# Gated attention and Mish MLP on one core: dense products as four tiles of 32 weight columns instead of one of 128

## The chip, the cores and the metric

The kernel runs on one core of a Trainium2 chip. The metric is device time in microseconds (us) of one execution, as the median over several runs. A core has TensorE (PE in the profile), VectorE (DVE), ScalarE (ACT), GpSimd (POOL) and SyncE (SP, which here issues DMAs). TensorE multiplies a stationary operand, which a weight load brings in, with a moving operand, and writes to eight banks of PSUM; VectorE and ScalarE read PSUM.

## What is computed

One token sequence of S = 2048 with D = 640 goes through 32-head attention (20 numbers a head, no mask) and through a two-layer MLP with Mish (F = 1536). A gate from a dot product mixes the two.

```python
g = _sigmoid((x * gate_w).sum(-1, keepdims=True))
qkv = x @ wqkv                      # split into q, k, v of 32 heads of 20
p = softmax(q @ k.T * 20 ** -0.5)   # per head, 2048 x 2048
a = (p @ v, heads side by side) @ wo
h = x @ w1 + b1
b = (h * tanh(softplus(h))) @ w2    # Mish
return g * a + (1 - g) * b
```

(The lines are condensed; shapes are x 2048x640, wqkv 640x1920, wo 640x640, w1 640x1536, w2 1536x640, all bf16.)

## The kernel before

**Groups and scores.** The attention is cut into 32 groups: a group is one set of four heads (eight of these) by one block of 512 queries (four of these). A group has 16 key tiles of 128 keys. The scores of one head, one key tile and one query block are one matmul of 32 rows (20 used) by 128 keys by 512 queries, one PSUM bank large (`score`, line 1081). The four heads stand at four row positions of the array, so up to four such matmuls run beside each other: the array is used as four tiles of 32 rows. There are 2048 of them.

**Exponentials.** Most score tiles go to ScalarE, two or three banks in one instruction, which writes bf16 into the ring `E` (line 1131). For some key tiles VectorE makes the exponential instead: from a score it computes an integer that is read as bf16 (`power`, line 444, one per head), and two shifted copies of that (`shift`, line 468, one instruction for four heads). The three are averaged by the product with V: the shifted copies meet V times a constant (`VD`, made on line 385 for the last `ND` key tiles). Such a key tile, a "D set", costs VectorE four powers and two shifts, and takes two ScalarE instructions' worth of work away.

**Product with V.** The probabilities of one key tile times V are four matmuls (`emit_pv`, line 1174), one per head: 128 keys by 21 columns of V (20 and a one for the row sum) by 512 queries. They stand at four column positions, so the array is used as four tiles of 32 columns. All accumulate in bank 7. A plain key tile has one such set of four, a D set three. The same tiling is used by filler matmuls with zero weights (`heat`, line 1410), which the planner puts where it finds TensorE idle and its recent activity low.

**Dense products.** The Q and K projections (`dense_chain`, line 577; `first_k_mm`, line 552), V with the gate (`v_chain`, line 662), the MLP's first layer (`h_chain`, line 724) and second layer (`b_chain`, line 789) and the output projection (`wo_chain`, line 870) use the whole 128x128 array: one weight load of 128 columns and one matmul of 81, 240, 320 or 512 moving columns for each 128 of contraction. Each is cut into a chain of such pieces into one free PSUM bank, followed by an evacuation on VectorE. A `Chain` has a start and a due time in units of groups. Mish runs on ScalarE in two large instructions (line 776).

**Order.** All instructions are issued in an order that a planner in the kernel writes out while it is built. It keeps a clock for each of PE, ACT and DVE with costs for each operation (`MM` = 216 ns for a matmul of 512 columns, `SWITCH` = 100 ns for a change of kind on TensorE). At each step `step_pe` chooses between scores (S, from `emit_s` and `d_unit`), a V set (`go_v`), a piece of a dense chain (`go_f`), filler (`heat`) and nothing. `mode` holds the kind that TensorE did last, and `switch` charges `SWITCH` for any other kind. Limits such as how many D sets may be ahead (`LEAD`), how many V sets must be ready (`VMIN`, `PVMAX`), how far behind its due work the dense part may fall (`BEHIND`), or the activity under which filler is put in (`HEAT`) come from `rule`, and `PLAN` sets them anew for each of the 32 groups. `NTS` counts the buffers for D sets and their shifts. The order is fixed in the program: on the chip each engine goes through its list and waits on semaphores.

```python
if mode[0] == kind or mode[0] is None:
    return 0.0
return SWITCH
```

**Tail.** After the last V set, bank 7 is transposed on VectorE and normalised (lines 1195 to 1222), 24 matmuls finish the last four output tiles (line 1573), and four stores end the kernel.

Of the kernel before, what the change touches and what calls it, by code (L numbers as in the profile page):

```python
# [20 lines left out]
class Chain:  # L21


    def __init__(self, start, due, pieces, evac, ready=None, before=None):
        self.start, self.due = start, due
        self.pieces = deque(pieces)
        self.evac = evac
        self.ready = ready or (lambda t: True)
        self.before = before
        self.cost = sum(c for c, _ in pieces)  # L30
# [32 lines left out]
def kernel(  # L63
# [36 lines left out]
    ND = 6  # L100
# [4 lines left out]
    VDUE = 0.13  # L105
    VA0 = 0.8
    VA1 = 0.8
    VB0 = 0.0
# [5 lines left out]
    OC = 1.6  # L114
    OD = 2.6
    OA = 1.4
# [4 lines left out]
    NTS = 9  # L121
# [36 lines left out]
    rule.HROOM = 0.0  # L158
    rule.WAIT1 = 0.0
# [3 lines left out]
        0.0: {'AHEAD': 5000.0, 'D2': 0.5, 'DQ': 1, 'DQ3': 2, 'DQ4': 2, 'ETIGHT': 0, 'HEAT': 0.9, 'LEAD': 6, 'LOW': 0.5, 'MARGIN': 30.0, 'NOPEN': 3, 'PVMAX': 4, 'Q3': 2, 'ROOM': 200.0, 'SWTH': 380.0, 'VMIN': 3, 'WAIT1': 2000.0, 'WAIT2': 6000.0, 'WAITU': 0.0},  # L163
        1.0: {'DQ': 1, 'DQ3': 2, 'HROOM': 0.0, 'LEAD': 5, 'WAIT1': -2000.0},
        2.0: {'DQ': 2, 'DQ3': 2, 'DQ4': 0, 'ETIGHT': 1, 'HEAT': 0.7, 'HROOM': 0.0, 'LOW': 0.38, 'MARGIN': 0.0, 'NOPEN': 3, 'Q3': 3, 'VMIN': 3, 'WAIT1': 2000.0, 'WAIT2': 100000.0},
        3.0: {'AHEAD': 1000.0, 'D2': 0, 'DQ3': 3, 'DQ4': 2, 'ETIGHT': 1, 'HROOM': -100.0, 'LEAD': 6, 'NOPEN': 3, 'WAIT1': 2000.0},
        4.0: {'AHEAD': 1000.0, 'ETIGHT': 1, 'HEAT': 0.8, 'HROOM': 100.0, 'KEEP3': 2, 'LOW': 0.56},
        5.0: {'AHEAD': 5000.0, 'D2': 0.5, 'DQ': 1, 'DQ3': 1, 'DQ4': 3, 'HEAT': 0.8, 'HROOM': 100.0, 'LEAD': 6, 'LOW': 0.56, 'MARGIN': 30.0, 'NOPEN': 4, 'PVMAX': 4, 'Q3': 3, 'SWTH': 380.0, 'WAIT1': 0.0, 'WAIT2': 6000.0},
        6.0: {'AHEAD': 5000.0, 'DQ3': 3, 'DQ4': 3, 'ETIGHT': 0, 'MARGIN': 100.0, 'NOPEN': 3, 'WAIT1': 0.0, 'WAIT2': 30000.0},
        7.0: {'DQ': 1, 'DQ3': 2, 'DQ4': 2, 'ETIGHT': 0, 'HEAT': 0.8, 'LOW': 0.6, 'MARGIN': 0.0, 'NOPEN': 3, 'ROOM': 300.0, 'SWTH': 300.0, 'WAIT1': 0.0, 'WAIT2': 100000.0},  # L170
        8.0: {'AHEAD': 2000.0, 'BEHIND': 6000.0, 'D2': 0.5, 'HEAT': 0.9, 'LOW': 0.44, 'NOPEN': 4, 'SWTH': 380.0, 'WAIT1': 2000.0, 'WAIT2': 30000.0},
        9.0: {'AHEAD': 2000.0, 'BEHIND': 6000.0, 'D2': 1.0, 'DQ3': 0, 'DQ4': 0, 'ETIGHT': 0, 'LOW': 0.56, 'MARGIN': 0.0, 'ROOM': 200.0, 'WAIT2': 100000.0},
        10.0: {'AHEAD': 5000.0, 'D2': 0.5, 'DQ3': 1, 'DQ4': 1, 'ETIGHT': 0, 'KEEP3': 3, 'LOW': 0.41, 'PVMAX': 3, 'SWTH': 520.0, 'WAIT1': -2000.0, 'WAIT2': 6000.0, 'WAITU': 0.0},
        11.0: {'D2': 0.5, 'DQ': 1, 'DQ3': 2, 'HEAT': 0.8, 'NOPEN': 4, 'PVMAX': 2, 'Q3': 2, 'VMIN': 3, 'WAIT1': 0.0, 'WAITU': 0.0},
        12.0: {'AHEAD': 1000.0, 'DQ': 1, 'DQ3': 3, 'DQ4': 0, 'HEAT': 0.9, 'MARGIN': 0.0, 'Q3': 2, 'ROOM': 200.0, 'SWTH': 520.0, 'WAIT2': 100000.0},
        13.0: {'AHEAD': 2000.0, 'BEHIND': 3000.0, 'DQ3': 2, 'ETIGHT': 0, 'HEAT': 0.8, 'KEEP3': 2, 'LOW': 0.47, 'PVMAX': 3, 'SWTH': 380.0, 'WAIT2': 6000.0, 'WAITU': 0.0},
        14.0: {'AHEAD': 2000.0, 'BEHIND': 2000.0, 'D2': 0, 'DQ4': 3, 'ETIGHT': 0, 'HEAT': 0.7, 'MARGIN': 60.0, 'WAIT1': -2000.0, 'WAIT2': 3000.0},
        15.0: {'AHEAD': 5000.0, 'D2': 0.5, 'DQ': 1, 'DQ3': 2, 'DQ4': 1, 'ETIGHT': 0, 'HEAT': 0.9, 'HROOM': 0.0, 'KEEP3': 1, 'LOW': 0.53, 'MARGIN': 60.0, 'NOPEN': 4, 'PVMAX': 2, 'SWTH': 380.0, 'WAIT2': 6000.0},
        16.0: {'AHEAD': 1000.0, 'D2': 1.0, 'DQ': 1, 'DQ3': 3, 'HEAT': 0.9, 'LEAD': 6, 'MARGIN': 30.0, 'PVMAX': 3, 'Q3': 2, 'SWTH': 380.0, 'WAITU': 0.0},
        17.0: {'AHEAD': 1000.0, 'D2': 0.5, 'DQ': 2, 'DQ4': 0, 'HEAT': 0.8, 'KEEP3': 3, 'LEAD': 6, 'NOPEN': 4, 'ROOM': 100.0},  # L180
        18.0: {'AHEAD': 2000.0, 'D2': 0.5, 'DQ': 1, 'DQ3': 0, 'DQ4': 3, 'HROOM': 0.0, 'LEAD': 6, 'LOW': 0.38, 'MARGIN': 0.0, 'PVMAX': 2, 'Q3': 3, 'ROOM': 200.0, 'SWTH': 380.0, 'VMIN': 3, 'WAIT2': 6000.0},
        19.0: {'BEHIND': 6000.0, 'DQ': 1, 'DQ3': 0, 'ETIGHT': 0, 'HROOM': 100.0, 'LEAD': 4, 'LOW': 0.38, 'MARGIN': 0.0, 'NOPEN': 4, 'ROOM': 300.0, 'WAIT1': -2000.0, 'WAIT2': 6000.0, 'WAITU': 0.0},
        20.0: {'AHEAD': 1000.0, 'BEHIND': 4000.0, 'DQ': 1, 'DQ3': 0, 'DQ4': 3, 'HROOM': 0.0, 'KEEP3': 2, 'LEAD': 5, 'LOW': 0.41, 'MARGIN': 30.0, 'NOPEN': 4, 'PVMAX': 3, 'ROOM': 200.0, 'SWTH': 380.0, 'VMIN': 3, 'WAIT1': -2000.0},
        21.0: {'AHEAD': 5000.0, 'D2': 1.0, 'DQ': 1, 'DQ4': 0, 'ETIGHT': 1, 'LOW': 0.5, 'ROOM': 100.0, 'WAIT1': -2000.0, 'WAIT2': 100000.0, 'WAITU': -200000.0},
        22.0: {'AHEAD': 5000.0, 'D2': 1.0, 'HEAT': 0.8, 'KEEP3': 3, 'LOW': 0.41, 'PVMAX': 2, 'Q3': 3, 'WAIT1': 0.0, 'WAIT2': 3000.0},
        23.0: {'AHEAD': 1000.0, 'BEHIND': 4000.0, 'D2': 0.5, 'DQ': 1, 'DQ3': 0, 'DQ4': 3, 'LOW': 0.53, 'NOPEN': 4, 'PVMAX': 3, 'SWTH': 380.0, 'VMIN': 3, 'WAIT1': -2000.0, 'WAIT2': 30000.0},
        24.0: {'AHEAD': 3000.0, 'DQ': 2, 'DQ3': 1, 'ETIGHT': 1, 'KEEP3': 3, 'LOW': 0.6, 'NOPEN': 4, 'PVMAX': 2, 'Q3': 2, 'SWTH': 380.0, 'WAIT1': 0.0, 'WAIT2': 30000.0, 'WAITU': -200000.0},
        25.0: {'DQ': 2, 'DQ3': 2, 'DQ4': 2, 'ETIGHT': 0, 'KEEP3': 3, 'LEAD': 6, 'LOW': 0.56, 'MARGIN': 100.0, 'NOPEN': 3, 'PVMAX': 3, 'WAIT1': -2000.0, 'WAIT2': 30000.0, 'WAITU': 0.0},
        26.0: {'AHEAD': 3000.0, 'BEHIND': 4000.0, 'D2': 0, 'DQ': 2, 'ETIGHT': 1, 'MARGIN': 0.0, 'NOPEN': 4, 'WAITU': 0.0},
        27.0: {'D2': 1.0, 'DQ': 2, 'DQ4': 1, 'HEAT': 0.8, 'HROOM': -200.0, 'KEEP3': 1, 'LOW': 0.6, 'MARGIN': 100.0, 'ROOM': 100.0, 'WAIT2': 30000.0, 'WAITU': 0.0},  # L190
        28.0: {'AHEAD': 1000.0, 'D2': 0.5, 'DQ': 1, 'HEAT': 0.8, 'HROOM': 0.0, 'LEAD': 5, 'LOW': 0.6, 'MARGIN': 30.0, 'ROOM': 300.0, 'VMIN': 3, 'WAIT1': 0.0, 'WAIT2': 30000.0, 'WAITU': -200000.0},
        29.0: {'AHEAD': 1000.0, 'HEAT': 0.9, 'HROOM': 100.0, 'LOW': 0.6, 'ROOM': 300.0, 'VMIN': 3, 'WAITU': -200000.0},
        30.0: {'AHEAD': 5000.0, 'BEHIND': 4000.0, 'D2': 1.0, 'DQ': 1, 'DQ3': 0, 'HEAT': 0.9, 'KEEP3': 3, 'LOW': 0.6, 'NOPEN': 4, 'PVMAX': 3, 'ROOM': 100.0, 'SWTH': 300.0, 'VMIN': 3, 'WAIT2': 100000.0, 'WAITU': -200000.0},
        31.0: {'AHEAD': 3000.0, 'HEAT': 0.9, 'KEEP3': 2, 'LOW': 0.6, 'PVMAX': 3, 'ROOM': 100.0},
# [305 lines left out]

    def transpose_chain(s, start, due):
# [20 lines left out]
        return Chain(start, due, [(420.0, piece)], evac, lambda t: t >= ARRIVE[c])  # L522
# [28 lines left out]
    def first_k_mm(ps, kt, c):  # L551
        nc.tensor.matmul(
            ps[:, :],
            lhsT=wkp[:, kt, :, :].rearrange("p h d -> p (h d)"),
            rhs=xT[:, kt, c * QC : (c + 1) * QC],
            start=(kt == 0),
            stop=(kt == KT - 1),
        )
# [10 lines left out]
    def dense_chain(kind, i, c, start, due):  # L569
# [4 lines left out]
        def piece(kt, t):  # L574
            if kt == 0:
                box["ps"] = bank_tile([P, QC])
            nc.tensor.matmul(  # L577
                box["ps"][:, :],
                lhsT=strips[(kind, i)][:, kt, :],
                rhs=xT[:, kt, c * QC : (c + 1) * QC],  # L580
                start=(kt == 0),
                stop=(kt == KT - 1),
            )
            if kt == KT - 1:
                strip_left[(kind, i)] -= 1
                if strip_left[(kind, i)] == 0 and i + 2 < 4 + (kind == 0):
                    load_strip(kind, i + 2, nc.sync)
# [67 lines left out]
    def v_chain(sts, w, c0, n, start, due, gate=False):  # L655
        width = n + (1 if gate else 0)

        def piece(k, t):
            i, kt = divmod(k, KT)
            if k == 0:  # L660
                box["ps"] = bank_tile([P, len(sts), width])
            nc.tensor.matmul(  # L662
                box["ps"][:, i, :],
                lhsT=xT[:, kt, sts[i] * P : (sts[i] + 1) * P],
                rhs=w[:, kt, c0 : c0 + width],
# [51 lines left out]
    def h_chain(ft, c, start, due):  # L717
        def piece(kt, t):
            if kt == 0:
# [4 lines left out]
            nc.tensor.matmul(  # L724
                box["ps"][:, :],
                lhsT=w1t[NW1 * c + ft // W1N][:, kt, (ft % W1N) * P : (ft % W1N + 1) * P],
                rhs=xT[:, kt, c * QC : (c + 1) * QC],
# [267 lines left out]
    def pick(t, any_start=False):  # L995
# [3 lines left out]
        for k, ch in enumerate(chains):  # L999
            if (any_start or ch.start <= prog[0]) and ch.ready(t):  # L1000
# [3 lines left out]
                if ch.before:  # L1004
                    ch.before()
# [624 lines left out]
```

## Time and profile before

| | us |
|---|---|
| median of 3 runs (lowest, highest) | 740.72 (740.61, 746.36) |
| the profiled execution | 739.59 |
| its span, first to last instruction | 737.8 |
| dense products, busy TensorE (by line: 789, 724, 577, 662, 870, 552) | 74.5, 65.0, 48.9, 34.0, 31.7, 4.0 |
| VectorE powers (line 444), 552 instructions | 363.7 |
| VectorE shifts (line 468), 276 instructions | 183.0 |
| Mish (line 776), 2 instructions, ScalarE | 20.9 |

The profile is of one execution. Busy time counts a stretch once in which instructions of one engine overlap; an instruction's mean duration is longer than the distance to the next one where they are pipelined, as matmuls (382 ns long, 216 ns apart) and exponentials are. A few per cent of the matmul records are missing: 204 of the 240 matmuls of line 724 are there, for instance. So counts are taken from the program and distances from pieces of the timeline that are whole.

### The profile page before, as it was taken

How to read it: one execution, taken by the hardware profiler on the slowest of the kernel's cores; microseconds unless marked ns; L12 is line 12 of the kernel's file. 1: busy time of each engine (PE TensorE's matmuls, PEld its weight loads, DVE VectorE, ACT ScalarE, POOL GpSimd, SP SyncE). 2: the span in 40 equal slices, each digit the busy share in tenths (PEclk: the TensorE clock that was granted, in tenths of full speed). 3: DMA queues.
4: the chain of work that ended last, by engine and by line, in shares of the span. 5: the costliest groups of instructions: out<-in, count | busy, mean ns of one | idle time of the engine just before them, and what ended most of it. 6: DMA issues, size and time to landing. Idle time of an engine off the chain costs nothing.

```text
span 737.8 us, 17000 instructions
## 1 busy us (share of the span) xinstructions
PE 714.6 (97%) x6669; PEld 231.8 (31%) x6725; DVE 664.8 (90%) x1180; ACT 718.0 (97%) x753; POOL 5.2 (1%) x12
## 2 busy tenths in 40 slices
PE   8999999999999999999999999999999999999996
PEld 4433222222222333333323222222233333333332
DVE  4488999998998899999888999999998999989986
ACT  5899999999999999999999999999999999999995
POOL 2000000000000000000000000000000000000000
PEclk9999999999999999999999999999999999999999
DMA  9511221224111210101221223311111212213231
GB/s 250 168 23 31 49 43 36 48 42 110 30 41 31 65 35 15 16 14 35 54 82 33 40 48 84 76 41 24 34 34 55 56 28 63 48 32 79 43 89 46
DMA packets 125584, 39.99 MB, mean 54 GB/s; under 512 B 91136, under 2 KB 124944, under 8 KB 125504
## 3 DMA queue, kind: packets, MB, share of 16 engines
q1 hardware_dynamic: 123616, 38.05, 22.7%
q8 instruction: 52, 0.85, 0.5%
q10 hardware_dynamic: 1888, 0.86, 0.4%
q14 instruction: 28, 0.23, 0.1%
HBM read 23.61 MB, written 12.79 MB: 49 GB/s over the span
## 4 chain that ended last, share of the span: by engine, by line
PE 46%; ACT 38%; issue 8%; DVE 5%; DMA 2%; SPq 1%; ACTq 0%; DVEq 0%
ACT E L1131 36%; PE Sp L1081 17%; PE Sp L1174 14%; PE Sp L789 6%; PE Sp L577 2%; DVE T L444 2%; PE Sp L724 2%; PE Sp L870 2%; ACT big L776 1%; DVE T L468 1%; PE Sp L662 1%; SPq L839 1%; DMA q_dram<-st 1%; DMA od<-o_dram 1%; DMA bl<-b_dram 0%
## 5 line engine op out<-in xcount | busy, mean ns | idle before, releaser
L1131 ACT ACTIVATE E<-Sp 128x1024 bf16<-128x1024 f32 (+1 forms) x737 | 686.9, 1123 | 4.6 <-PE Sp L1081 4.4
L444 DVE TENSOR_SCALAR T<-Sp 128x512 int16<-128x512 f32 x552 | 363.7, 681 | 37.3 <-PE Sp L1081 33.6
L1081 PE MATMUL Sp<-qT,kT 32*128 32x512 bf16 x2048 | 298.1, 383 | 8.5 <-ACT E L1131 2.8
L468 DVE TENSOR_SCALAR T<-T 128x2048 int16<-128x2048 int16 x276 | 183.0, 677 | 0.8 <-PE Sp L1174 0.4
L1081 PEld LDWEIGHTS <-kT 32*128 32x128 bf16 x2048 | 82.2, 91 | 276.6 <-issue 272.1
L1174 PE MATMUL Sp<-E,VA 128*21 128x512 bf16 x1496 | 137.7, 382 | 0.0
L1174 PE MATMUL Sp<-T,VD 128*21 128x512 bf16 x1104 | 102.4, 382 | 0.4 <-DVE T L468 0.3
L789 PE MATMUL Sp<-w_sb,big 128*128 128x320 bf16 x384 | 74.5, 302 | 0.0
L724 PE MATMUL Sp<-xT,w1t 128*128 128x512 bf16 x204 | 65.0, 383 | 4.0 <-issue 3.7
L1174 PEld LDWEIGHTS <-VA 128*21 128x21 bf16 x2048 | 41.2, 90 | 60.2 <-issue 48.9
L1174 PE MATMUL Sp<-T,VA 128*21 128x512 bf16 x552 | 51.7, 383 | 0.0
L577 PE MATMUL Sp<-xT,ws 128*128 128x512 bf16 x162 | 48.9, 383 | 1.6 <-issue 1.4
L789 PEld LDWEIGHTS <-big 128*128 128x128 bf16 x384 | 28.4, 97 | 33.4 <-issue 27.4
L743 DVE TENSOR_SCALAR big<-Sp,b1f 128x512 bf16<-128x512 f32 x48 | 35.4, 738 | 1.0 <-PE Sp L724 0.9
L1174 PEld LDWEIGHTS <-VD 128*21 128x21 bf16 x1104 | 26.2, 90 | 30.1 <-issue 22.9
L662 PE MATMUL Sp<-wv,xT 128*128 128x81 bf16 (+2 forms) x240 | 34.0, 258 | 0.7 <-DVE T L444 0.5
L870 PE MATMUL Sp<-wo_sb,od 128*128 128x320 bf16 (+1 forms) x152 | 30.5, 302 | 0.8 <-DVE big L890 0.4
L597 DVE CAST st<-Sp 128x512 bf16<-128x512 f32 x36 | 24.5, 682 | 4.4 <-DMA q_dram<-st 2.8
L1195 DVE STREAM_TRANSPOSE T<-Sp 128x512 f32<-128x512 f32 x32 | 22.7, 708 | 2.3 <-PE Sp L1174 2.3
L724 PEld LDWEIGHTS <-w1t 128*128 128x128 bf16 x240 | 15.5, 97 | 29.0 <-issue 26.5
L678 DVE CAST VA<-Sp 128x80 bf16<-128x80 f32 (+2 forms) x48 | 16.1, 372 | 8.6 <-PE Sp L662 8.6
L662 PEld LDWEIGHTS <-xT 128*128 128x128 bf16 x240 | 16.5, 98 | 16.7 <-issue 14.5
(69 smaller groups left out, 194.4 us busy)
## 6 DMA issues: line engine op xcount, KB each, us to landing
w1t<-in_B_w_dram SPq DMA_DIRECT2D x24, 320.0 KB
q_dram<-st SPq DMA_DIRECT2D x20, 128.0 KB
b_dram<-bt SPq DMA_DIRECT2D x16, 160.0 KB
bl<-b_dram SPq DMA_DIRECT2D x16, 160.0 KB
qT<-q_dram SPq DMA_DIRECT2D x124, 20.0 KB
o_dram<-T SPq DMA_DIRECT2D x120, 20.0 KB
kT<-k_dram SPq DMA_DIRECT2D x28, 80.0 KB
out_dram<-ot SPq DMA_DIRECT2D x14, 160.0 KB
```

The costliest lines, as they stand in the source:

```text
L444: nc.vector.tensor_scalar(out=d["T"][:, r * QC : (r + 1) * QC].bitcast(I16), in0=ps[:, :], scalar1=inv_sqrt_dh * LOG2E * 128.0, scalar2=12 ...
L468: nc.vector.tensor_scalar(out=tile_[:, :].bitcast(I16), in0=d["T"][:, :].bitcast(I16), scalar1=float(SHIFT[i]), scalar2=None, op0=ALU.add,)
L577: nc.tensor.matmul(box["ps"][:, :], lhsT=strips[(kind, i)][:, kt, :], rhs=xT[:, kt, c * QC : (c + 1) * QC], start=(kt == 0), stop=(kt == K ...
L597: nc.vector.tensor_copy(out=res["st"][:, :], in_=ps[:, :])
L662: nc.tensor.matmul(box["ps"][:, i, :], lhsT=xT[:, kt, sts[i] * P : (sts[i] + 1) * P], rhs=w[:, kt, c0 : c0 + width], start=(kt == 0), stop ...
L724: nc.tensor.matmul(box["ps"][:, :], lhsT=w1t[NW1 * c + ft // W1N][:, kt, (ft % W1N) * P : (ft % W1N + 1) * P], rhs=xT[:, kt, c * QC : (c + ...
L743: nc.vector.tensor_scalar(out=big[:, slot.tag, (ft % 2) * QC : (ft % 2 + 1) * QC], in0=ps[:, :], scalar1=b1f[:, ft : ft + 1], scalar2=None ...
L789: nc.tensor.matmul(box["ps"][:, :], lhsT=big[:, pair[(c, ft // 2)].tag, (ft % 2) * QC + u * P : (ft % 2) * QC + (u + 1) * P], rhs=w2_sb[:, ...
L870: nc.tensor.matmul(box["ps"][:, :], lhsT=od[c][0:r, k, u * P : (u + 1) * P], rhs=wo_sb[0][0:r, k, cols], start=(k == 0), stop=(k == n - 1),)
L1081: nc.tensor.matmul(ps_cols, lhsT=kT[p][32 * t_ : 32 * t_ + 32, j * P : (j + 1) * P], rhs=qT[G][32 * t_ : 32 * t_ + 32, :], tile_position=( ...
L1131: nc.scalar.activation(E[:, x : x + n, :], ps, ACT.Exp, scale=inv_sqrt_dh,)
L1174: nc.tensor.matmul(acc[32 * t_ : 32 * t_ + DH + 1, :], lhsT=lhsT, rhs=rhs, start=(pv_done[G] == 0), stop=(pv_done[G] == pv_total[G] - 1), ...
```

## The change

Each dense product is made of four matmuls at column positions 0, 32, 64 and 96, each with 32 columns of the weights and the same moving operand, as the V sets are. The six places that issued one matmul call the new `product`. The initial projections (line 1275), the transposes and the 24 matmuls of the tail keep the whole array; so the transposes' chain gets `col=False`.

The planner now keeps two things: the kind it did last, and the tiling that the array has (`tiles`). A dense piece and a V set have the same tiling and cost no switch between them; where both could go on, it prefers the kind it is in. The costs of the pieces in the planner are what they were. Some constants and the table `PLAN` are new: one fewer key tile per group has a `VD`, there is one more buffer for D sets, and starts and due times of a few chains move. `rule.VF` is 0 throughout. `before` of `Chain` was not used and goes.

```diff
-    ND = 6
+    ND = 5
...
-    VDUE = 0.13
+    VDUE = 0.16
...
-    VB0 = 0.0
+    VB0 = 0.5
...
-    OC = 1.6
-    OD = 2.6
-    OA = 1.4
+    OC = 0.8
+    OD = 1.8
+    OA = 1.2
...
-    NTS = 9
+    NTS = 10
...
+    rule.VF = 0
...
+    def product(out_, lhsT, rhs, **kw):
+
+        for k in range(0, P, 32):
+            nc.tensor.matmul(
+                out_[k : k + 32], lhsT=lhsT[:, k : k + 32], rhs=rhs, tile_position=(0, k), **kw
+            )
+
...
-            nc.tensor.matmul(
+            product(
                 box["ps"][:, :],
-                lhsT=big[:, pair[(c, ft // 2)].tag, (ft % 2) * QC + u * P : (ft % 2) * QC + (u + 1) * P],
-                rhs=w2_sb[:, ft, half * HALF : (half + 1) * HALF],
+                big[:, pair[(c, ft // 2)].tag, (ft % 2) * QC + u * P : (ft % 2) * QC + (u + 1) * P],
+                w2_sb[:, ft, half * HALF : (half + 1) * HALF],
                 start=(ft == 0),
                 stop=(ft == FT - 1),
             )
...
-    M1 = 30.0
+    M1 = 31.0
...
+    tiles = [None]
+
+    def tiling(kind):
+        if kind == "F":
+            return "V" if chain[0] is None or chain[0].col else "F"
+        return kind
+
     def switch(kind):
-        if mode[0] == kind or mode[0] is None:
-            return 0.0
-        return SWITCH
+        return 0.0 if tiles[0] in (None, tiling(kind)) else SWITCH
+
+    def enter(kind):
+        sw = switch(kind)
+        mode[0], tiles[0] = kind, tiling(kind)
+        return sw
...
         if units:
-            if mode[0] == "V" and n_pv and slack > MM:
-                return go_v()
-            if mode[0] == "F" and slack > MM and can_f(slack):
-                return go_f()
+            if slack > MM and mode[0] in ("V", "F"):
+                if n_pv and tiles[0] == "V" and (mode[0] == "V" or rule.VF):
+                    return go_v()
+                if can_f(slack) and switch("F") == 0.0:
+                    return go_f()
+                if n_pv and tiles[0] == "V":
+                    return go_v()
...
-        if mode[0] == "V" and n_pv:
+        if n_pv and tiles[0] == "V" and (mode[0] == "V" or rule.VF):
             return go_v()
         if end and n_pv and cur["G"] >= NG - 1:
             return go_v()
-        if mode[0] == "F" and can_f(slack):
+        if mode[0] in ("V", "F") and can_f(slack) and switch("F") == 0.0:
             return go_f()
+        if n_pv and tiles[0] == "V":
+            return go_v()
```

## The prediction

> **What bounds the kernel now.** I read the page first: how full each engine is, and the chain of waits.
>
> ```profile
> span 737.8 us, 17000 instructions
> PE 714.6 (97%) x6669; PEld 231.8 (31%) x6725; DVE 664.8 (90%) x1180; ACT 718.0 (97%) x753; POOL 5.2 (1%) x12
> PEclk9999999999999999999999999999999999999999
> PE 46%; ACT 38%; issue 8%; DVE 5%; DMA 2%; SPq 1%; ACTq 0%; DVEq 0%
> ```
>
> ScalarE and TensorE are both at 97%, and the chain goes to and fro between them. DVE has 73 us free, and the clock stands at full. A busy PE is not a PE at its peak, so I take distances from the timeline, in a stretch in mid-kernel where no record is missing (start, length, engine):
>
> ```profile
> 299.74 6.59 ACT L1131 ACTIVATE E<-Sp 128x1024 bf16<-128x1024 f32 x7
> ...
> 299.97 0.39 PE L1081 MATMUL Sp<-qT,kT 32*128 32x512 bf16 x2
> ...
> 300.29 0.40 PE L1174 MATMUL Sp<-E,VA 128*21 128x512 bf16 x4
> 300.30 0.10 PEld L1174 LDWEIGHTS <-VD 128*21 128x21 bf16 x4
> 300.51 0.39 PE L1174 MATMUL Sp<-T,VD 128*21 128x512 bf16 x4
> ...
> 300.73 0.39 PE L1174 MATMUL Sp<-E,VA 128*21 128x512 bf16 x4
> ...
> 301.05 0.39 PE L1081 MATMUL Sp<-qT,kT 32*128 32x512 bf16 x3
> ...
> 301.38 0.58 PE L789 MATMUL Sp<-w_sb,big 128*128 128x320 bf16 x3
> ...
> 303.08 0.72 PE L789 MATMUL Sp<-w_sb,big 128*128 128x320 bf16 x4
> ...
> 303.73 0.39 PE L1081 MATMUL Sp<-qT,kT 32*128 32x512 bf16 x3
> ```
>
> Seven exponentials span 6.59 us and the last takes 1.11, so their distance is (6.59 - 1.11)/6 = 0.913. Four matmuls of a V set run together, and set follows set at 0.22 (0.216 between the second and third of a stretch). From scores to V is 0.32, from V to scores 0.32 as well: 0.216 of work and 0.105 lost at a change of tiling. From a product back to scores, 303.08 to 303.73, is 0.65 for four pieces; pieces of 320 follow each other at (0.72 - 0.30)/3 = 0.14 (0.136 in the records), so 0.10 is lost there. A last view, the groups by shape, has the sizes of the exponentials:
>
> ```profile
> L1131 ACT ACTIVATE E<-Sp 128x1024 bf16<-128x1024 f32 x715 | 661.6, 1110 | 4.1 <-PE Sp L1081 3.9
> L1131 ACT ACTIVATE E<-Sp 128x1536 bf16<-128x1536 f32 x22 | 33.8, 1534 | 0.5 <-PE Sp L1081 0.5
> ```
>
> **The reserve of each engine before.** ScalarE runs exponentials from 10.6 to 727.7, 717.1 us. At 0.913, and 0.42 more for each wide one, 737 take 682; Mish with its table loads 26. So ScalarE loses only 9 us to waits.
> For PE I count the program's order: 748 stretches of scores x 0.321 = 240.1; 788 V and 48 filler sets x 0.216 = 180.6; 339 ways out of V x 0.105 = 35.6; products 435 x 0.216 + 616 x 0.136 + 80 x 0.102 + 80 x 0.040 = 189.2 (512, 320, 240, 81 columns); 409 ways out of products x 0.096 = 39.3; 6.5 for first sets, which are 7 to 10 ns longer; 3.4 of transposes. Together 694.7 of the 718.1 us from the first scores (10.2) to the end of the last V set: a reserve of 23 us, 3%, some 5 of it in the first 20 us. PE is nearly as tight as ScalarE.
>
> **The change, part by part.** Instructions are counted from the two built programs.
>
> *Exponentials.* 715 narrow and 22 wide become 700 and 28: nine fewer x 0.913, less six x 0.42 = **-5.7 us** of ScalarE. D sets go from 138 to 141 (powers 552 to 564, shifts 276 to 282).
>
> *VectorE.* 12 x 0.66 + 6 x 0.67 = +12 us on 664.8: 677 of some 733. Its 56 us of free time cover it; uncovered it would cost those 12. The smaller `VD` tiles (16 of 0.28) give back under 1. Nothing.
>
> *Tiling changes.* Products and V sets now stand next to each other 98 times instead of 18. But scores still come between most stretches, and all changes of tiling fall only from 1519 to 1476: 13 fewer stretches of scores, -4.2 us. The ways out of products now cost what they cost from V: 728 x 0.105 and 0.7 for transposes, against 35.6 + 39.3 before, +2.2. First sets -1.4.
>
> *V and filler.* 794 V sets, +1.3 us; 75 fillers, +5.8.
>
> *Products as four tiles.* 1211 pieces become 4844 matmuls, each with its own weight load. For 512 columns the V set is the row: 0.216, what the whole-array piece takes too. So nothing for 435 pieces. For 320, 240 and 81 no row has four tiles. From below: the moving columns alone, as today, +0 (a gain is excluded, as a piece can't stream in less than its columns). From above: eight instructions in a row, one load and one matmul at the closest distance that the trace shows kept up, 0.040 (pieces of 81 columns: eight in 0.48, the last 0.20). Four pairs are 0.156 to 0.160: +20 ns x 616, +54 x 80, +116 x 80 = 12.3 + 4.3 + 9.3 = +26 us. I take +0 to +3: in a V set the four matmuls start 3 ns apart, so pairs can be issued far closer than 40 ns, and the row of four loads at 300.30 ends within 0.10, under the 0.136 of a piece of 320. Only the 80 pieces of 81 columns, before 50 us, should get longer.
>
> [...]
>
> *PE in all.* -4.2 + 2.2 - 1.4 + 1.3 + 5.8 = +3.7: 698.4 us with products as long as before.
>
> *Tail.* Before, the last exponential (726.6 to 727.7) ends just ahead of the last V set (728.12), and the end comes 10 us later. In the new order a power (0.66), two shifts (1.3) and a V set (0.4) stand behind the last exponential's start: some 2.9 us to the transpose of bank 7 instead of 1.95. **+1 us**. Thirteen more pieces of the output projection stand there too (1.8 us), beside VectorE's 2.8 us of normalising.
>
> DMAs are the same in number; the programs' 7,500 more PE instructions are more to fetch, on queues that moved 1.08 MB in 0.6% of the DMA engines' time. Nothing.
>
> *What is late next.* The span from first scores to last V shrinks to 718.1 - 5.7 + 1.0 = 713.4, and PE needs 698.4 of it: a reserve of 15 in place of 23. ScalarE's waits of 9 us come from scores that PE brings late. Left as they are they add nothing; grown in inverse proportion to the reserve they are 14, +5. I take +2.
>
> Sum: 739.6 - 5.7 + 1.0 + 2.0 = 736.9, on the profiled execution, whose 739.6 lies 1.1 under the median of the runs. Forecast **737 us**.
>
> **The rivals.**
> 1. *Four-tile products take longer, and PE sets the time* (slower). Place: the 776 pieces under 512 columns. For: no row shows eight PE instructions in 0.136 us, and PE's reserve is small. Against: starts 3 ns apart in V sets. It decides from where PE's reserve of 15 falls under some 8 us, +7 us, or 11 ns per piece of 320. At the bound of +26, PE's 724.3, the 10.2 before, a reserve of 5 to 15, the tail of 11 and the 1.8 outside the span make 752 to 762; at half of it 742. So 742 to 762, 750 in the middle.
> 2. *The gain is eaten by PE's thinner reserve*: waits grow by 5 or more, and the V sets of three more D sets come late: 740 to 743. For: PE's sum rises though its time shrinks. Against: 5.8 of the rise is filler, put where the planner found PE idle.
> 3. *Waits fall as well*: the freer order meets ScalarE's needs better; without half of its waits 739.6 - 5.7 + 1.0 - 4.5 = 730.4, so 730 to 734. For: 98 places without a drain. Against: the counts of changes hardly move.
> 4. *Weight loads show at each entry* (slower). 0.10 for four loads, at the 424 entries into products, is +42: 780. Against: V sets have such entries, 300.29 to 300.51, and lose 7 ns. [...]
>
> **How the numbers follow.** Forecast (734 to 740): 0.55. Rival 1: 0.19; rival 2: 0.11; rival 3: 0.12; rival 4: 0.03. From 731 (into rival 3) to 752 (rival 1 up to just past its middle) some 0.13 is left out; the range is 731 to 752, and the forecast's own is 734 to 740. One per cent, about what a measurement of this kernel can tell from no change, is 7.4: faster means under 733.3, slower over 748.1. Faster: most of rival 3 and the forecast's edge, 0.16. Slower: 0.6 of rival 1, rival 4, and 0.04 for late D sets on VectorE, 0.18. Same: 0.66.
>
> **What would show it.** Exponentials' distance 0.913 again, and ScalarE's busy time down by 5 to 6. Pieces of 320 at 0.136 between sets; at 0.145 or more rival 1 begins, and PE's waits vanish while ScalarE's grow. 0.32 from a product's last set to scores, and no drain between a product and a V set. An entry of 0.22 to the second set speaks against rival 4. The forecast is wrong if the granted clock falls under full anywhere in mid-kernel, which no row of before leads me to expect, or if DVE, at over 92%, begins to hold V sets.

## The result, and the profile after

| | before | after |
|---|---|---|
| median of the runs made side by side, us (lowest, highest) | 741.55 (740.41, 747.87), 20 runs | 745.76 (741.83, 748.33), 20 runs |
| ratio after / before, 95% interval | | 1.0036 [1.0019, 1.0053] |
| profiled execution, us | 739.59 | 743.93 |
| its span, us | 737.8 | 742.1 |

The kernel became 4.2 us slower by the medians, where 2.7 us faster was forecast; by the interval of the ratio, which is not that of the medians, the loss is 1.4 to 3.9 us. The profiled executions differ by 4.3 us, so the two profiles may stand for the difference of the medians, though each lies about 2 us under its own median. Of after's 20 runs 12 had a mean granted clock of 0.995 or less, the profiled one 0.997; where such a run loses the rest is not known, as none was profiled. The head of the page of after (span; busy time of each engine; granted clock in 40 slices; the chain of waits by engine):

```profile
span 742.1 us, 24594 instructions
...
PE 724.0 (98%) x10490; PEld 235.8 (32%) x10490; DVE 673.3 (91%) x1198; ACT 712.8 (96%) x744; POOL 5.2 (1%) x12
...
PEclk9999999999999999999999999999999999999999
...
PE 84%; ACT 9%; DVE 4%; issue 2%; DMA 1%; ACTq 0%; DVEq 0%; SPq 0%
```

ScalarE (ACT) is busy 5.2 us less than before, as forecast, and the span is 4.3 longer: 9.5 us of new waiting on ScalarE. The chain no longer goes to and fro between PE and ScalarE (46% and 38% before); 84% of it is PE. The groups by shape show the new mixture of exponentials, and behind each the idle time ahead of it:

```profile
L1139 ACT ACTIVATE E<-Sp 128x1024 bf16<-128x1024 f32 x700 | 648.2, 1099 | 8.1 <-PE Sp L1089 7.0 <-PE Sp L1182 1.1
L1139 ACT ACTIVATE E<-Sp 128x1536 bf16<-128x1536 f32 x28 | 42.2, 1512 | 4.3 <-PE Sp L1089 4.3
```

That idle time was 4.1 + 0.5 us before and is 8.1 + 4.3 now. Three lines from the list of waits say what is behind it (engine, line, what it waited for; sum, times, longest, in us):

```profile
ACT E L1139 <- PE Sp L1089: 11.3, 7, 4.7
...
DVE st L607 <- DMA q_dram<-st: 5.0, 1, 5.0
...
PE Sp L1089 <- DVE st L607: 3.3, 1, 3.3
```

These are few and long waits, seven for ScalarE with one of 4.7 us, and not many short ones from a PE that is a little late everywhere. Before had the same three kinds in small: 4.4, 2.8 and 0.4 us.

**The first place** is around 255 us, under the first of the two Mish instructions (250.4 to 260.9, ScalarE busy with it). The timeline of after (start, length, engine, instruction; in brackets the idle time before and what ended it):

```profile
251.07 1.91 SPq L1239 DMA_DIRECT2D o_dram<-T  x4
...
252.24 0.69 DVE L607 CAST st<-Sp 128x512 bf16<-128x512 f32 x1 [0.39 <-PE Sp L505]
...
253.08 0.43 SPq L610 DMA_DIRECT2D q_dram<-st  x1
...
255.39 0.39 PE L1089 MATMUL Sp<-qT,kT 32*128 32x512 bf16 x3
258.38 1.29 DVE L607 CAST st<-Sp 128x512 bf16<-128x512 f32 x2 [4.97 <-DMA q_dram<-st]
...
259.13 0.37 PE L1089 MATMUL Sp<-qT,kT 32*128 32x512 bf16 x1 [3.35 <-DVE st L607]
```

A finished Q or K projection goes from its bank into one of two staging buffers `st` (line 607) and from there to memory (line 610). VectorE wants to copy a third projection, finds both buffers still on their way out, and stands for 4.97 us; its instructions run in the order of the program, so the powers behind that copy stand too, banks stay full, and PE stands for 3.35 us. The store issued at 253.08 was slow, landing 5.2 us later: four stores of attention output (`o_dram`, packets of 40 bytes, issued from 251.07) are ahead of it. Before issued those 1.6 us earlier, at 249.47, and its projection store at 252.67 landed after 2.7 us. In both kernels the projection's store lands 0.5 to 0.9 us behind the last of the four (257.79 and 258.27 in after, 254.42 and 255.35 before). That the four themselves took 6.7 us from the first issue to the last landing, and 5.0 before, is not explained by any run. In three stretches around this place (length; busy time and instructions of PE, of PEld, which is its weight loads, of DVE, ACT and POOL; granted clock; DMA share; GB/s):

```profile
252.00:255.00 3.00, 3.00 (x68) 1.69 (x67) 1.17 (x2) 3.00 (x1) 0.00 (x0) 1.00 0.85 84
255.00:258.40 3.40, 0.78 (x15) 0.10 (x4) 0.01 (x1) 3.40 (x1) 0.00 (x0) 1.00 0.37 31
258.40:262.00 3.60, 2.87 (x29) 1.18 (x32) 3.07 (x5) 3.58 (x2) 0.00 (x0) 0.69 0.23 68
```

In the first the DMA engines are 85% taken; in the second PE and VectorE stand; in the third the granted clock is 0.69. Looked at closely it is 0.50 from 259.80 to 263.21, for 3.41 us. The clock row of the page, in slices of 18.6 us, does not show this.

**The second place** is under the second Mish instruction (538.0 to 548.5):

```profile
547.38 0.72 PE L505 MATMUL Sp<-wo_sb,od 128*32 128x320 bf16 x16
...
548.82 1.68 PE L505 MATMUL Sp<-wo_sb,od 128*32 128x320 bf16 x44 [0.72 <-DMA od<-o_dram]
...
551.28 1.01 DVE L900 SCALAR_TENSOR_TENSOR ot<-Sp,g_t,bl 128x320 bf16<-128x320 f32 x2 [2.33 <-DMA bl<-b_dram]
551.88 0.86 PE L505 MATMUL Sp<-wo_sb,od 128*32 128x320 bf16 x20 [1.38 <-DVE ot L900]
...
553.58 1.03 ACT L1139 ACTIVATE E<-Sp 128x1024 bf16<-128x1024 f32 x1 [1.84 <-PE Sp L1089]
```

The output projection reads attention output that five transposing loads bring back (`od`, line 849). It is ordered before they have landed (`od`: 0.72 us), and its evacuation before the rows of `b` are there (`bl`: 2.33 us); ScalarE comes out of Mish and waits. The longest gap of PE is 1.38 us here, and in this profile the granted clock stays at 1.00 (a stretch as above):

```profile
547.00:553.00 6.00, 3.90 (x97) 2.50 (x96) 3.67 (x8) 4.71 (x4) 0.00 (x0) 1.00 0.49 129
```

So the span's +4.3 us is put together like this, from the start times of the exponentials and scores in the two traces:

| part | forecast | measured |
|---|---|---|
| first exponential | 0 | +0.2 |
| exponentials at their closest spacing (0.904 us narrow, 1.331 wide, in both kernels) | -5.7 | -5.6 |
| ScalarE's waits | +2 | +8.3 |
| from the last exponential to the end (10.04 to 11.46 us) | +1 | +1.4 |

The 8.3 us have places: 4.25 after the first Mish, 1.95 after the second, 1.25 at 202.5 us and 0.8 at 34.3 us, where eight and ten V sets and product sets stand in a row without scores. So 6.2 us of them stand behind late transfers, and 2.0 us behind the new order itself.

### The profile page after: what moved, and what is told of

Read it like the earlier page. It is cut to its first block, busy times and chain, and to the rows that moved or that the text cites. A ratio compares the mean times of both kernels' runs of the same rounds, so it can differ in the third digit from the quotient of the medians.

```text
span 742.1 us, 24594 instructions
## 1 busy us (share of the span) xinstructions
PE 724.0 (98%) x10490; PEld 235.8 (32%) x10490; DVE 673.3 (91%) x1198; ACT 712.8 (96%) x744; POOL 5.2 (1%) x12
## 4 chain that ended last, share of the span: by engine, by line
PE 84%; ACT 9%; DVE 4%; issue 2%; DMA 1%; ACTq 0%; DVEq 0%; SPq 0%
PE Sp L1089 29%; PE Sp L505 27%; PE Sp L1182 24%; ACT E L1139 8%; PE Sp L1426 2%; DVE T L445 2%; DVE T L469 1%; DMA q_dram<-st 1%; DMA bl<-b_dram 0%; PE Sp L322 0%; DVE st L607 0%; PE Sp L1594 0%; PE Sp L1283 0%; PE Sp L515 0%; PE Sp L1259 0%
## 5 line engine op out<-in xcount | busy, mean ns | idle before, releaser
L1139 ACT ACTIVATE E<-Sp 128x1024 bf16<-128x1024 f32 (+1 forms) x728 | 681.8, 1115 | 12.4 <-PE Sp L1089 11.3
L445 DVE TENSOR_SCALAR T<-Sp 128x512 int16<-128x512 f32 x564 | 370.2, 683 | 31.0 <-PE Sp L1089 29.2
L505 PE MATMUL Sp<-w_sb,big 128*32 128x320 bf16 x1536 | 76.1, 302 | 0.0
L505 PE MATMUL Sp<-xT,w1t 128*32 128x512 bf16 x960 | 74.7, 384 | 0.1
L505 PE MATMUL Sp<-xT,ws 128*32 128x512 bf16 x720 | 54.6, 390 | 0.3 <-DVE T L445 0.3
L505 PEld LDWEIGHTS <-big 128*32 128x32 bf16 x1536 | 30.4, 95 | 32.0 <-issue 27.4
L505 PE MATMUL Sp<-wv,xT 128*32 128x81 bf16 (+2 forms) x960 | 33.4, 258 | 0.0
L505 PE MATMUL Sp<-wo_sb,od 128*32 128x320 bf16 (+1 forms) x608 | 29.5, 302 | 2.1 <-DVE ot L900 1.4
L1426 PE MATMUL Sp<-xT,zero_w 128*21 128x512 bf16 x300 | 29.3, 392 | 0.0
L505 PEld LDWEIGHTS <-w1t 128*32 128x32 bf16 x960 | 17.5, 94 | 29.1 <-issue 26.2
L505 PEld LDWEIGHTS <-xT 128*32 128x32 bf16 x960 | 17.8, 96 | 13.3 <-issue 11.1
```

What stands on the lines that cost most here:

```text
L445: nc.vector.tensor_scalar(out=d["T"][:, r * QC : (r + 1) * QC].bitcast(I16), in0=ps[:, :], scalar1=inv_sqrt_dh * LOG2E * 128.0, scalar2=12 ...
L505: nc.tensor.matmul(out_[k : k + 32], lhsT=lhsT[:, k : k + 32], rhs=rhs, tile_position=(0, k), **kw)
L1139: nc.scalar.activation(E[:, x : x + n, :], ps, ACT.Exp, scale=inv_sqrt_dh,)
L1426: nc.tensor.matmul(acc[32 * t_ : 32 * t_ + DH + 1, :], lhsT=zero_w[:, 0 : DH + 1], rhs=xT[:, 0, 0:QC], start=False, stop=False, tile_posit ...
```

## The experiments

Each ratio is to the kernel before on the same chip (medians 741.3 to 741.4 there), with its 95% interval. The theories at the start: the products as four tiles cost time; or the new order does, by its late transfers; or it does by PE's thin reserve, a little everywhere.

### The change in halves

The products alone, with the planner, constants and order of before; all six places are edited in this way:

```diff
-            nc.tensor.matmul(
+            product(
                 box["ps"][:, :],
-                lhsT=w1t[NW1 * c + ft // W1N][:, kt, (ft % W1N) * P : (ft % W1N + 1) * P],
-                rhs=xT[:, kt, c * QC : (c + 1) * QC],
+                w1t[NW1 * c + ft // W1N][:, kt, (ft % W1N) * P : (ft % W1N + 1) * P],
+                xT[:, kt, c * QC : (c + 1) * QC],
```

> The order, the constants and the planner of before; only the six dense products are made of four matmuls of 32 weight columns. Theory A (the tiles themselves cost nothing, and the changed kernel loses by its new order, at a few places where a transfer holds up VectorE and TensorE): pieces of 320 stay at 0.136 us, the way out of a product grows by 9 ns (409 times, 3.7 us of TensorE, mostly in its reserve), the granted clock stays at 1.0; 741 to 743 us, ratio to before 1.000 to 1.003. Theory B (the tiles cost, by their weight loads, their 7,500 more instructions or a lower granted clock): as slow as the changed kernel or slower, 745 to 750, ratio 1.004 or more, clock under 0.998.

Measured: 744.10 us (741.65 to 746.24), ratio 1.0029 [1.0008, 1.0050], between the ranges of the two theories.

The order alone: after with whole-array products.

```diff
     def product(out_, lhsT, rhs, **kw):
-        for k in range(0, P, 32):
-            nc.tensor.matmul(
-                out_[k : k + 32], lhsT=lhsT[:, k : k + 32], rhs=rhs, tile_position=(0, k), **kw
-            )
+        nc.tensor.matmul(out_, lhsT=lhsT, rhs=rhs, **kw)
```

> The order of the changed kernel, with each dense product as one matmul of the whole array again; so products and V sets that stand next to each other pay a change of tiling. Theory A: the stall near 255 us (TensorE idle for over 3 us, then the clock at half) stays, and 98 neighbourhoods cost 0.1 us each where they were free, less 9 ns at some 360 ways out: +7 us of TensorE against the changed kernel, of which its small reserve hides part; 748 to 753. Theory B: the whole-array products take the cost away; under 743.

Measured, in five runs: 748.92 us (746.74 to 749.63), ratio 1.0090 [1.0057, 1.0122]. It has the same two places, with waits of 4.4 us for a staging buffer and 3.5 us for `bl`; so neither the tiles nor their 7,500 more instructions make these waits.

What follows: either half alone is slower than before, and the halves do not add (2.9 and 9.0 thousandths, 3.6 together). Given the new order, four tiles are the better products. In the profile of the first half the losses are mostly not spread either: of the 3.8 us by which its last scores are behind those of before, 3.0 stand at four points, ahead of the first scores (0.5), at the first Mish (0.8), at a late `od` load at 628 us (1.0) and near 709 us (0.8).

### More staging buffers

```diff
-    NST = 2
+    NST = 4
```

> The changed kernel with four staging buffers instead of two for the Q and K projections; every instruction is in the same place. Theory A: VectorE no longer waits 5 us for the store of a staging buffer near 254 us, TensorE's idle stretch of 3.4 us shrinks under 1, the clock does not fall to half there, and ScalarE's wait of 4.8 us after Mish falls under 1.5: 3 to 5 us less, 741 to 743, clock 0.998 or more. Theory B: the tiles' cost is everywhere; no change, 744 to 747.

> The kernel before with four staging buffers instead of two, the same order. Theory A: the same place costs the kernel before 2.8 us of VectorE and 0.6 of ScalarE only; 0 to 1 us less, ratio 0.998 to 1.000. Theory B says nothing here; if it gains as much as the changed kernel does (3 us or more), the staging buffers explain none of the difference between the two.

After with four buffers: 741.51 us (739.24 to 743.51), ratio 0.9990 [0.9971, 1.0009]. Before with four: 739.83, ratio 0.9974 [0.9946, 1.0002], an interval that takes in 1. So the staging buffers account for about 4 of after's 745.8, with everything on ScalarE and VectorE in the same order. The profiled execution (743.51 us, mean clock 0.992) is the longest of the twelve, and so shows more loss than the median. In it VectorE's wait at the first Mish is down to 0.17 us; the second place has grown:

```profile
537.02 6.42 SPq L849 DMA_TRANSPOSE od<-o_dram  x5
...
547.49 4.46 PE L505 MATMUL Sp<-wo_sb,od 128*32 128x320 bf16 x64 [3.28 <-DMA od<-o_dram]
```

Five transposing loads take 6.42 us to issue on one queue, and the last has landed 10.5 us after the first issue. The planner counts 8 us from that issue (`o_ready`, line 854), so PE is sent into a wait of 3.28 us. The half clock comes with it, here from 545.80, 1.6 us into that gap of PE, for 6.83 us:

```profile
545.80:552.63 6.83, 5.14 (x76) 2.81 (x76) 2.88 (x6) 2.03 (x3) 0.00 (x0) 0.50 0.25 87
```

The 64 matmuls (16 pieces) at 547.49 take 4.46 us; at full clock, 0.136 a piece, they would take some 2.3. The five runs of this kernel at a full mean clock took 739.2 to 739.6, the seven with a lower one 741.3 to 743.5.

### The second place by itself

With two staging buffers as in after, the output projection is put as late as it was before:

```diff
-    OC = 0.8
-    OD = 1.8
+    OC = 1.6
+    OD = 2.6
```

> The changed kernel with the output projection's start and due time of before (OC 1.6 and OD 2.6 instead of 0.8 and 1.8), two staging buffers; the planner writes a new order from the second half on. Theory A2 (the second place of loss is the output projection that is due inside the second Mish, before its transposed attention output has landed): no TensorE gap over 1 us between 530 and 560 us, no half clock there; the stall near 255 us stays; 1 to 3 us under the changed kernel, 743 to 745. Rival (the loss is spread over the new order): no change, 745 to 747.

Measured: 746.32 us (742.74 to 749.41), ratio 1.0041 [1.0012, 1.0069]: a miss. The wait under the second Mish is gone, but the first is there (4.5 us), and a new one has come into the tail, where PE waits 2.98 us for `big`, which waits for a `bl` load, and the last 16 matmuls behind that wait then take 3.89 us, against 2.34 for the same 16 in after. Moving the projection moves the wait, and the time is that of after.

Alternatively the planner is told a later landing:

```diff
-        o_ready[qc] = t + 8000.0
+        o_ready[qc] = t + 12000.0
```

> The changed kernel, but the planner counts 12 us instead of 8 from the issue of the transposed loads of the attention output to their use; the starts are as in the changed kernel. Theory A2: as with the later start, the gap at 540 to 560 us goes, 743 to 745; if only the later start helps and this does not, the collision is with something else in that window than the loads. Rival: no change, 745 to 747.

Measured: 744.11 us (742.24 to 746.37), ratio 1.0012 [0.9988, 1.0036], about 1.6 under after by the medians. The intervals overlap, so the times alone do not show a gain; the profile does show that the second wait is gone and no new one comes, while the first stays (4.2 us). Here too the order is a new one from the second half on.

### Products in the old order, and fillers

The first half again, with four staging buffers (`NST = 4`):

> The order of before with products as four tiles, and four staging buffers. Theory C (TensorE paces the kernel, so the 9 ns more at each of 409 ways out of a product, less 3 at each entry, come through): 2 to 3 us over the kernel before with four staging buffers (739.8), 742 to 743. Theory A alone (tiles cost only where they make a transfer late): the staging buffers take it away, 740 to 741.

Measured: 744.15 us (741.17 to 745.83), ratio 1.0010 [0.9984, 1.0036]. Both theories missed: by the median nothing was gained over two buffers. The profile says why the time is not PE's pace: against before with four buffers the scores fall back by only 0.7 us in 600, and then lose 2.9 us at one place, where PE waits 1.97 us for `od` (629.50) and then runs at half clock (stretches as above):

```profile
626.80:630.10 3.30, 1.33 (x26) 0.45 (x27) 1.69 (x4) 1.65 (x2) 0.00 (x0) 1.00 0.59 68
630.10:633.51 3.41, 3.41 (x32) 0.71 (x33) 1.84 (x3) 2.45 (x3) 0.00 (x0) 0.50 0.39 109
```

The stores ahead of those loads took 3.17 us to issue instead of 1.95, so the loads began late. That is one profile; how often the runs meet it was not measured.

Next, after with four staging buffers and without its 75 filler sets (matmuls with zero weights that add zero to bank 7 are left out):

```diff
-            for t_ in range(4):
-                nc.tensor.matmul(
-                    acc[32 * t_ : 32 * t_ + DH + 1, :],
-                    lhsT=zero_w[:, 0 : DH + 1], rhs=xT[:, 0, 0:QC], start=False, stop=False,
-                    tile_position=(0, 32 * t_), skip_group_check=True,
-                )
```

> The changed kernel with four staging buffers and without its 75 filler sets: the planner counts them as before but issues none, so all else stands in the same order. The output is the same, as they add zero. Theory C (fillers stand in TensorE's way): 75 x 0.216 = 16 us of TensorE go, of which those outside the waits come through, 3 to 6 us under the kernel with fillers (741.5), 736 to 739. Rival 1 (they fill waits): 741 to 742. Rival 2 (they keep the clock up): clock under 0.99 and over 743.

Measured: 740.21 us (739.08 to 746.18), ratio 0.9976 [0.9946, 1.0006]. The best run is 0.16 us from the best with filler (739.24), so the fillers' time does not come through. But they are not without use: no run without them had a mean clock over 0.998, and five of the twelve with them had 1.000. Of the runs without them three had a clock under 0.99, and these took over 744 us (744.1, 744.7, 746.2), as rival 2 said; the profiled one had 0.989. The two effects were not separated.

### Both mends, and the change taken apart again

Two more staging buffers, which are those of the output tiles (`ot0`, `ot1`), and 12 us for the loads:

```diff
-    stages = [Slot(f"st{i}") for i in range(NST)]
+    stages = [Slot(tag) for tag in ("st0", "st1", "ot0", "ot1")]
...
-        o_ready[qc] = t + 8000.0
+        o_ready[qc] = t + 12000.0
```

They go into after, into before with the products alone, into before itself, and into after with whole-array products (the edit of the second half). The planner writes each order anew with them, so from the second half on the order is not that of after, or of before, with the waits taken out. The two kernels with the same planner and constants have the same order.

> The changed kernel with both places mended: four staging buffers (two of them in the space of the output tiles ot0 and ot1, which are idle then), and 12 us instead of 8 counted for the transposed loads. Theory A2 (the two stalls and the half clock after each are what put it behind): 4 us less for the first, 1.7 for the second, 739.5 to 741, clock 0.998 or more in most runs, ratio to before 0.996 to 1.000. Rival (something else of the order is slow as well): 742 or more.

> The planner and constants of before, products as four tiles, both places mended. Against the next-but-one kernel of this batch, which differs in the tiles alone: theory A2 (tiles cost nothing but 9 ns a way out, mostly hidden): 0 to 1 us more. Theory C (all of it comes through): 2 to 3 us more.

> The kernel before with both places mended, whole-array products. The staging buffers gave 1.6 us; its waits for the transposed loads are 0.4 us in its profile: 739 to 740.5, ratio 0.996 to 0.999. If it is as fast as the mended changed kernel, the change itself is worth nothing here; if 2 us slower, the mixed order is worth that.

> The mended changed kernel's order with whole-array products, so the neighbourhoods of products and V sets pay 0.1 us again, as in the run of the order alone, which was 3 us over the changed kernel: 743 to 745 against some 740. If it is equal to the mended changed kernel, tiles are worth nothing even where the order mixes both kinds.

| with both mends, us, ratio to before | whole-array products | four tiles |
|---|---|---|
| planner and constants of before | 739.59, 0.9976 [0.9960, 0.9991] | 740.11, 0.9983 [0.9967, 0.9998] |
| planner and constants of after | 743.44, 1.0023 [1.0004, 1.0042] | 740.05, 0.9973 [0.9955, 0.9991] |

After with both mends has a span of 739.0 us at a mean granted clock of 1.0. The same stretches at the first Mish, and one at the second:

```profile
252.00:255.00 3.00, 3.00 (x68) 1.73 (x64) 2.13 (x4) 3.00 (x1) 0.00 (x0) 1.00 0.37 24
255.00:258.40 3.40, 3.40 (x64) 1.57 (x60) 2.70 (x5) 3.40 (x1) 0.00 (x0) 1.00 0.86 121
258.40:262.00 3.60, 3.60 (x48) 0.95 (x36) 3.52 (x6) 3.60 (x1) 0.00 (x0) 1.00 0.20 63
```

```profile
547.00:553.00 6.00, 5.81 (x96) 2.08 (x92) 5.54 (x10) 6.00 (x8) 0.00 (x0) 1.00 0.11 31
```

PE works through all of them; in after it worked 0.78 of the 3.40 us and 3.90 of these 6.00. ScalarE's waits for scores are 4.9 us in place of 11.3. What follows from the table:

- The two waits, with the half clock that came with them in some profiles (0.50 for 3.41 us in after, for 6.83 us with four staging buffers), are after's loss against before: without them it is 740.05 in place of 745.76, at the interval of 0.9955 to 0.9991 beside 1.0019 to 1.0053. About 4 of the 5.7 us came with the staging buffers alone and the order unchanged; the rest came with a new order as well.
- Four tiles in the old order cost 0.5 us by the medians, which the intervals cannot tell from nothing. In the mixed order they are worth 3.4 us, and there the intervals do not meet: whole-array products pay the change of tiling between products and V sets that this order makes often. In the two profiles the 70 such neighbourhoods found between 60 and 700 us are 0.10 us longer with whole-array products (0.32 us in place of 0.22 at 512 columns), 7 us of PE, of which about half comes through.
- The change as a whole, old order with whole-array products to new order with tiles, is +0.46 us: nothing that the intervals tell from zero. The mends gain 1.7 us in before and 5.7 in after, and bring the two to the same time; the fastest median is that of before with both.

## Why the prediction failed

**The products as four tiles: right.** Records of after in a whole stretch give 216 ns from set to set for 512 columns, 136 for 320, 102 to 103 for 240, and 39 for 81. These are the whole-array distances. The timeline has the narrowest and the 320 ones:

```profile
22.26 0.57 PE L505 MATMUL Sp<-wv,xT 128*32 128x81 bf16 x40
...
249.18 0.85 PE L505 MATMUL Sp<-wv,xT 128*32 128x320 bf16 x20
```

Ten sets of 81 in 0.57, the last 0.20 long: 0.04 apart. Five of 320 in 0.85, the last 0.30: 0.14. The upper bound of +26 us (rival 1) was built on pairs at 40 ns; four pairs run in 39 ns. Rival 4's 0.10 us at each entry is not there: the first set of a product behind scores is 10 ns longer than the next, 226 against 216 at 512 columns. Even the caution of +0 to +3 was not needed.

**Changes of tiling: right.** The last set of a product to scores is 321 ns, and a product next to a V set has no loss:

```profile
441.89 0.40 PE L1089 MATMUL Sp<-qT,kT 32*128 32x512 bf16 x4
...
442.22 0.40 PE L505 MATMUL Sp<-xT,w1t 128*32 128x512 bf16 x4
...
442.44 0.39 PE L1182 MATMUL Sp<-T,VD 128*21 128x512 bf16 x4
...
442.77 0.39 PE L1089 MATMUL Sp<-qT,kT 32*128 32x512 bf16 x2
```

0.22 from the product to the V set, 0.33 from that back to scores.

**ScalarE's work and the tail: right.** -5.7 forecast, -5.6 measured; +1 forecast, +1.4 measured. **VectorE: right that it covers its share.** It is busy 8.5 us more, where I counted 12, and at 91% V sets wait for it for 0.3 us in all.

**ScalarE's waits: the step that failed.** "Left as they are they add nothing; grown in inverse proportion to the reserve they are 14, +5. I take +2." They grew by 8.3. The size is not the main fault; the mechanism is. I took ScalarE's waits for a smooth function of PE's reserve, as if PE were a little late everywhere. 6.2 us of the growth stand at two places at which a transfer is late, and a reserve of 15 or 23 us, spread over 700, is no help against 3.4 us at one point. The other 2.0 us are as many as I forecast, but that is luck: they too stand at two points, behind rows of sets without scores, and not in proportion to a reserve. The second step that failed is "Nothing" for the DMAs. Rival 2 had the right sign for the wrong reason: it too went by the mean reserve, and its ceiling of 743 was too low. No V set had to wait for a D set of VectorE. The time fell into rival 1's range without rival 1's mechanism, so it is luck as well that the stated range of 731 to 752 holds it.

The prediction said that it would be wrong "if the granted clock falls under full anywhere in mid-kernel, which no row of before leads me to expect". It fell in after's profile, for 3.41 us, behind the gap at the first Mish. And the rows were there, though for the cause and not for the clock: before's timeline had, at the same copy into the staging buffer,

```profile
255.47 1.29 DVE L597 CAST st<-Sp 128x512 bf16<-128x512 f32 x2 [1.49 <-DMA q_dram<-st]
...
258.08 0.69 DVE L597 CAST st<-Sp 128x512 bf16<-128x512 f32 x1 [1.33 <-DMA q_dram<-st]
```

Two waits of 1.3 to 1.5 us on two buffers cost the profiled execution of before nothing that shows (its span is that of before with both mends); in the medians the mends gain 1.7 us. I read the change's new start times (`OC`, `OD`) and new order for what PE does, and said of the DMAs "the same in number … Nothing". Their number is the same; their order against the copies is not.

**What stays open.** After with both mends has less exponential work than before with both (693 narrow and 35 wide against 724 and 17: 4.0 us less by the closest spacing), and is no faster. By the start times of the exponentials in the two profiles, its first exponential comes 0.7 us later, its waits are 2.5 us longer, nearly all before 45 us and at 203 us, where the rows of sets without scores stand, and from the last exponential to the end it takes 2.0 us more; with the 4.0 less that makes the 1.2 us between the two spans. So even without the two late transfers the forecast gain of 2.7 us is not there. No run took these away one by one.

## What to carry to other kernels

- Before a change of order is costed, list in the old profile the waits that end on a transfer (here 1.5 us, for a buffer of which there are two) and ask what the new order puts ahead of that transfer. A mean reserve says nothing about a point.
- A gap in PE's work can cost twice: its own length, and a half clock after it (in after 3.35 us, and 3.41 us at 0.50), which a clock row in coarse slices (18.6 us) hides. Ask for the clock in short stretches behind every place where PE waits for a transfer.
- When a change does two things, try each with the other's accidents mended: 1.0029, 1.0090 and 1.0036 looked like a costly order, and became 0.5 us of products and nothing for the whole.

## What was not expected of the hardware

- Four column tiles, each with its own load of 32 columns, kept up with one whole-array piece down to 81 moving columns: 39 ns for four loads and four matmuls, where the whole-array piece took 40.
- Idle gaps of PE from 2.0 us (1.97 at 629.50, with the old order, four tiles and four staging buffers; PE was busy for 1.33 of the 3.30 us there) to 3.4 us came with a granted clock of 0.50 for 3.41 or 6.83 us: behind the gap in two of the three profiles, and from 1.6 us into a gap of 3.28 in that of after with four staging buffers. The run of the order alone slows down in the same way with no gap over 1 us just ahead: three pieces of the output projection take 0.58 us at 550.54, and three at 553.31 take 0.98, behind gaps of 0.94 and 0.95 us. After's second place, with a gap of 1.38 us, had no such fall; what decides between them stays open.
- A store issued 2.0 us behind four stores in 40-byte packets took 5.2 us to land, against 2.7 us when it was issued 3.2 us behind them.
